# Attention scores in bursts of six PSUM banks instead of four, two bursts per head group

## The chip, the cores and the metric

One core of one Trainium2 chip. The metric is the device time of one execution in microseconds (us), the slowest (here the only) core, as the median of several runs.

## The reference

One transformer block, sequence 2048, width 1024, 32 heads of 32, a sliding window of 256 keys, bfloat16:

```python
q, k, v = split(layernorm(x) @ wqkv)                     # 32 heads of width 32
scores  = einsum("bhqd,bhkd->bhqk", q, k) * 32 ** -0.5
p       = softmax(where(0 <= q_idx - k_idx < 256, scores, -1e9))
h       = x + einsum("bhqk,bhkd->bhqd", p, v) @ wo
out     = h + silu(layernorm(h) @ w1) @ w2               # w1: 1024x3584, w2: 3584x1024
```

## The kernel before

The sequence is worked in four blocks of 512 queries. The attention of one block runs between the dense matmuls of the next one (its v, q and k projections; for the last block the output projection). Heads go in eight groups of four; the four heads of a group lie in the four 32-row tiles of the array (row tiles), which run at once: in the trace their four first score matmuls start within 0.01 us. A group needs 12 chunks of 128 keys by 128 queries per head, done in three bursts of four chunks:

```python
PIECES = {                                  # key tile, first query tile, how many, chunk
    "A": [(0, 0, 3, 0), (-2, 0, 1, 3)],
    "B": [(-1, 0, 2, 0), (2, 2, 2, 2)],
    "C": [(3, 3, 1, 0), (1, 1, 3, 1)],
}
def scores(b, g, kind):
    for kt, q0, nq, ch in PIECES[kind]:
        for hh in range(4):                 # four row tiles, each with a bank of its own
            r0 = hh * DH
            nc.tensor.matmul(sc[hh // 2][:, hh % 2, ch*P:(ch+nq)*P], lhsT=kT[...][r0:r0+DH, ...],
                             rhs=qT[b][r0:r0+DH, ...], start=True, stop=True, tile_position=(r0, 0))
    for pair in range(2):                   # one exponential per two heads: 1024 columns
        nc.scalar.activation(out=e, in_=sc[pair], func=ACT.Exp, scale=scale)
        ...                                 # masks on GpSimd
# ... per group g and kind:
    scores(b - 1, g, kind)
    dense[n]()                              # eight matmuls of 512 columns
    pending.pop(0)()                        # a third of the previous group's value matmuls
```

The kernel's PSUM tiles fill eight banks: four for scores, two accumulators, two for value outputs.

The softmax here doesn't subtract the row's maximum and nothing guards it: scores larger than these inputs give would overflow.

## Time and profile before

| what | measured |
|---|---|
| time, median of 3 | 696.83 us (696.65 to 697.57) |
| TensorE busy | 690.1 us, 99% of the span |
| one burst, first score to next dense matmul | 0.33 us |
| one head group (three dense groups, three bursts, 48 value matmuls), median | 7.68 us |
| bursts | 18 in the first attention block, 72 later |

In the profile's lines PE is TensorE's matmuls, PEld its weight loads, DVE VectorE, ACT ScalarE, POOL GpSimd. Read the timeline of TensorE by the starts: the end of a matmul is modelled, and one matmul lies over the next.

### The profile page before, as it was taken

How to read it: one execution, taken by the hardware profiler on the slowest of the kernel's cores; microseconds unless marked ns; L12 is line 12 of the kernel's file. 1: busy time of each engine (PE TensorE's matmuls, PEld its weight loads, DVE VectorE, ACT ScalarE, POOL GpSimd, SP SyncE). 2: the span in 40 equal slices, each digit the busy share in tenths (PEclk: the TensorE clock that was granted, in tenths of full speed). 3: DMA queues.
4: the chain of work that ended last, by engine and by line, in shares of the span. 5: the costliest groups of instructions: out<-in, count | busy, mean ns of one | idle time of the engine just before them, and what ended most of it. 6: DMA issues, size and time to landing. Idle time of an engine off the chain costs nothing.

```text
span 695.5 us, 12334 instructions
## 1 busy us (share of the span) xinstructions
PE 690.1 (99%) x5091; PEld 331.6 (48%) x5091; DVE 289.5 (42%) x616; ACT 257.9 (37%) x328; POOL 174.5 (25%) x391
## 2 busy tenths in 40 slices
PE   8999999999999999999999999999999999999998
PEld 3444444555555555544444444444444444444445
DVE  6267646644443448544316134433133251244111
ACT  4326657777777777621310023300033100233000
POOL 1007667777777777500000000000000000000000
PEclk9999999999999999999999999999999999999999
DMA  7732131026231778880123410024200023100110
GB/s 241 257 53 77 35 93 51 17 60 193 70 124 23 205 251 272 199 311 31 31 76 99 107 38 1 1 83 77 83 1 1 11 95 91 45 1 1 30 39 24
DMA packets 76457, 60.84 MB, mean 87 GB/s; under 512 B 50288, under 2 KB 60528, under 8 KB 76400
## 3 DMA queue, kind: packets, MB, share of 16 engines
q1 hardware_dynamic: 76256, 59.78, 29.9%
q8 instruction: 40, 0.66, 0.4%
q10 hardware_dynamic: 144, 0.26, 0.1%
q14 instruction: 17, 0.14, 0.1%
HBM read 39.85 MB, written 8.39 MB: 69 GB/s over the span
## 4 chain that ended last, share of the span: by engine, by line
PE 99%; DMA 1%; DVE 0%; issue 0%
PE hacc L563 19%; PE hacc L600 17%; PE acc L248 16%; PE acc L600 10%; PE acc L563 9%; PE acc L238 8%; PE acc L267 7%; PE o_ps L339 4%; PE sc L285 3%; PE hacc L267 1%; PE o_ps L354 1%; PE sc L313 1%; DMA r_o<-in_A_x_dram 1%; PE tp L216 0%; DVE ln_st L169 0%; DVE r_o L197 0%
## 5 line engine op out<-in xcount | busy, mean ns | idle before, releaser
L330 POOL TENSOR_SCALAR_AFFINE_SELECT r_e<-r_e 128x256 bf16<-128x256 bf16 (+1 forms) x384 | 171.6, 477 | 116.5 <-ACT r_e L322 65.1
L293 ACT ACTIVATE r_e<-sc 128x1024 bf16<-128x1024 f32 x144 | 139.5, 1021 | 45.1 <-PE sc L285 31.0
L600 PEld LDWEIGHTS <-r_a 128*128 128x128 bf16 x952 | 90.9, 98 | 103.0
L563 PEld LDWEIGHTS <-r_w 128*128 128x128 bf16 x896 | 87.4, 98 | 104.8
L600 PE MATMUL hacc<-r_a 128*128 128x512 bf16 (+2 forms) x616 | 122.5, 360 | 0.0
L563 PE MATMUL hacc<-r_e,r_w 128*128 128x512 bf16 x456 | 100.9, 379 | 0.0
L572 ACT ACTIVATE r_n<-hacc 128x512 f32<-128x512 f32 x30 | 17.9, 597 | 178.9 <-PE hacc L563 178.9
L600 PE MATMUL acc<-r_a 128*128 128x512 bf16 x336 | 74.0, 379 | 0.0
L248 PEld LDWEIGHTS <-r_w 128*128 128x128 bf16 x512 | 46.5, 97 | 57.1 <-issue 7.0
L250 DVE CAST r_a<-acc 128x512 bf16<-128x512 f32 x56 | 38.7, 691 | 72.9 <-PE acc L248 56.3
L248 PE MATMUL acc<-r_t,r_w 128*128 128x512 bf16 x256 | 60.0, 379 | 0.0
L248 PE MATMUL acc<-r_w 128*128 128x512 bf16 x256 | 58.2, 380 | 0.0
L267 PE MATMUL acc<-r_o,r_a 128*128 128x512 bf16 x208 | 49.4, 380 | 0.0
L563 PE MATMUL acc<-r_e,r_w 128*128 128x512 bf16 x216 | 49.1, 379 | 0.0
L339 PEld LDWEIGHTS <-r_e 128*128 128x128 bf16 x1152 | 39.5, 96 | 17.0
L322 ACT ACTIVATE r_e<-sc 128x1024 bf16<-128x1024 f32 x36 | 34.9, 1021 | 21.2 <-PE sc L313 20.1
L339 PE MATMUL o_ps<-r_a,r_e 128*128 128x33 bf16 x1152 | 40.2, 178 | 0.0
L615 DVE SCALAR_TENSOR_TENSOR r_t<-hacc,r_t 128x512 bf16<-128x512 f32 (+2 forms) x22 | 14.0, 635 | 56.7 <-PE hacc L600 56.7
L267 PEld LDWEIGHTS <-r_a 128*128 128x128 bf16 x256 | 23.1, 98 | 29.6 <-issue 5.1
L615 DVE SCALAR_TENSOR_TENSOR r_t<-acc,r_t 128x512 bf16<-128x512 f32 x12 | 8.3, 692 | 64.2 <-PE acc L600 64.2
L573 DVE SCALAR_TENSOR_TENSOR r_a<-r_n,hacc 128x512 bf16<-128x512 f32 x30 | 20.6, 688 | 33.0 <-ACT r_n L572 33.0
L563 PE MATMUL hacc<-r_a,r_w 128*128 128x512 bf16 x144 | 32.9, 379 | 0.0
(71 smaller groups left out, 476.5 us busy)
## 6 DMA issues: line engine op xcount, KB each, us to landing
r_w<-in_B_w_dram SPq DMA_DIRECT2D x8, 896.0 KB, 5.1
r_a<-in_B_w_dram SPq DMA_DIRECT2D x7, 1024.0 KB, 7.9
r_w<-in_A_wqkv_dram SPq DMA_DIRECT2D x6, 1024.0 KB, 8.7
h_dram<-r_t SPq DMA_DIRECT2D x16, 256.0 KB, 3.0
r_t<-h_dram SPq DMA_DIRECT2D x16, 256.0 KB, 2.8
out_dram<-r_t SPq DMA_DIRECT2D x31, 128.0 KB, 1.7
r_o<-in_A_x_dram SPq DMA_DIRECT2D x15, 256.0 KB, 4.0
r_e<-h_dram SPq DMA_DIRECT2D x3, 1024.0 KB, 5.7
```

What stands on the lines that cost most here:

```text
L238: nc.tensor.matmul(acc, lhsT=lnT_b[b % 2][:, kt, j * P:(j + 1) * P], rhs=wv[:, kt, c * 512:(c + 1) * 512], start=(kt == 0), stop=(kt == KT ...
L248: nc.tensor.matmul(acc, lhsT=wqk[:, kt, col0:col0 + P], rhs=lnT_b[b % 2][:, kt, :], start=(kt == 0), stop=(kt == KT - 1))
L250: copy(out=(qT, kT)[which][b][:, g, :], in_=acc)
L267: nc.tensor.matmul(acc, lhsT=qT[b][:, g, j * P:(j + 1) * P], rhs=wo[:, g, c * 512:(c + 1) * 512], start=(g == 0), stop=(g == G - 1))
L285: nc.tensor.matmul(sc[hh // 2][:, hh % 2, ch * P:(ch + nq) * P], lhsT=kT[t // 4][r0:r0 + DH, g, (t % 4) * P:(t % 4 + 1) * P], rhs=qT[b][r0 ...
L293: nc.scalar.activation(out=e, in_=sc[pair], func=ACT.Exp, scale=scale)
L322: nc.scalar.activation(out=e, in_=sc[pair], func=ACT.Exp, scale=scale)
L330: nc.gpsimd.affine_select(out=ap, in_=ap, pattern=[[0, 2], [0, n], [sgn, P]], compare_op=ALU.is_ge if upper else ALU.is_gt, fill=0.0, base ...
L339: nc.tensor.matmul(o_ps[pair][:, qt * 2 + hh, 0:VW], lhsT=e_of(i, kind, pair)[:, hh, ch * P:(ch + 1) * P], rhs=v[:, b * 4 + kt, g * 4 + pa ...
L563: nc.tensor.matmul(acc, lhsT=w1[:, kt, ft * P:(ft + 1) * P], rhs=ln2T[b][:, kt, :], start=(kt == 0), stop=(kt == KT - 1))
L600: nc.tensor.matmul(acc[:, 0:c1 - c0], lhsT=gT[:, ft, j * P:(j + 1) * P], rhs=w2[ft // 4][:, ft % 4, c0:c1], start=(ft == 0), stop=(ft == F ...
L615: nc.vector.scalar_tensor_tensor(out=t_out[j % 2][:, c0:c1], in0=acc[:, 0:c1 - c0], scalar=0.5, in1=t_in[j % 2][:, c0:c1], op0=ALU.mult, o ...
```

## The change

Its intent: every burst pays for switching the array into four row tiles and back, so fewer and longer bursts should cost less. A burst becomes six chunks per head (768 columns). The fifth and sixth go into half banks: heads 0 and 1 share the accumulator bank that is not in use, heads 2 and 3 one auxiliary bank taken from the value outputs. The design holds that two row tiles must not write one bank at once, so within a burst the odd heads write their halves first and the even heads last. What enforces it are two tiny "mark" matmuls: each takes a new tile of a pool with one buffer, so the second mark gets a semaphore wait (a semaphore is a counter that one instruction steps and another waits for) for the completion of the first.

```diff
+PIECES = [[(0,0,3,0), (-2,0,1,3), (-1,0,2,4)], [(3,3,1,0), (1,1,3,1), (2,2,2,4)]]
-    if not bursts or len(bursts[-1]) == 4:
+    if not bursts or len(bursts[-1]) == 6:
+    half = [acc[:, 0:256], acc[:, 256:512], flat[:, 0:256], flat[:, 256:512]]
+    for hh in range(4):
+        at = 0
+        for p in (aux + own[::-1] if hh % 2 else own):      # odd heads: auxiliary first
+            todo.append((at, 1 - hh % 2, hh, p)); at += p[4]
+    todo.sort(key=lambda t: t[:3])
+    def mark(hh):
+        nc.tensor.matmul(o_tile()[:, 0, 0:4], lhsT=ident[r0:r0+DH, :], rhs=ident[r0:r0+DH, 0:4],
+                         start=True, stop=True, tile_position=(r0, 0))
+    for _, _, hh, p in todo:
+        if hh == 1 and p[5] < 4 and not marked:
+            mark(1); marked = True
+        score(hh, p)
+    mark(0)
+    for p in aux:
+        for hh in (0, 2):                                   # even heads: auxiliary last
+            score(hh, p)
+    exp(ea[:, 0:2, :], acc); exp(em[:, 0, :], sc[0][:]); exp(em[:, 2, :], sc[2][:])
+    exp(ea[:, 2:4, :], flat); exp(em[:, 1, :], sc[1][:]); exp(em[:, 3, :], sc[3][:])
 ... (cut: masks on four heads at once, one value output bank in place of two, value matmuls
 ...  in two pieces per group, bursts after the 7th and 4th matmul of a dense group,
 ...  layernorm statistics in half steps)
```

## The prediction

> **What bounds the kernel now.** I read the engine totals first, then the chain of waits that ended last, then the timeline inside one attention stage. The totals and the chain by line:
>
> ```profile
> PE 690.1 (99%) x5091; PEld 331.6 (48%) x5091; DVE 289.5 (42%) x616; ACT 257.9 (37%) x328; POOL 174.5 (25%) x391
> ...
> PE 99%; DMA 1%; DVE 0%; issue 0%
> ```
>
> TensorE (PE) is never without a matmul in flight and the chain is PE from end to end. So only PE's own stream counts, plus any new wait put into it. But "busy" also covers the drain of the array between kinds of matmul, so the timeline must tell what is stream and what is drain. One iteration of the output-projection stage, with ScalarE beside it:
>
> ```profile
> 242.06 0.40 PE L285 MATMUL sc<-r_a 32*128 32x128 bf16 x8
> ...
> 242.39 1.90 PE L267 MATMUL acc<-r_o,r_a 128*128 128x512 bf16 x8
> ...
> 242.58 1.94 ACT L293 ACTIVATE r_e<-sc 128x1024 bf16<-128x1024 f32 x2 [0.67 <-PE sc L285]
> ...
> 244.13 0.54 PE L339 MATMUL o_ps<-r_a,r_e 128*128 128x33 bf16 x15
> ...
> 244.60 0.40 PE L285 MATMUL sc<-r_a 32*128 32x384 bf16 x8
> ```
>
> Columns: start and duration in us, engine, line, operation, how many. Read starts, not durations: the ends are modelled. Scores to dense group: 0.33 us. Eight dense matmuls to the value matmuls: 1.74 us, so 0.216 each. Fifteen value matmuls to the next scores: 0.47 us. The piece after 290.16 (value matmuls, then dense at 290.54) has the same fifteen in 0.38 us, so one value matmul costs 0.025 us and the way from full-array work into the scores costs about 0.09 us. The scores stream 512 columns on each of four row tiles at once; at the dense rate that is 0.213 us, so the way out of the scores costs 0.33 - 0.213 = 0.12 us. The first attention block, where scores interrupt a dense stream, agrees:
>
> ```profile
> 59.83 2.53 PE L238 MATMUL acc<-r_w,r_t 128*128 128x512 bf16 x11
> ...
> 62.29 0.40 PE L313 MATMUL sc<-r_a 32*128 32x128 bf16 x12
> ...
> 62.63 0.62 PE L354 MATMUL o_ps<-r_a,r_e 128*128 128x33 bf16 x18
> ...
> 63.09 2.53 PE L238 MATMUL acc<-r_w,r_t 128*128 128x512 bf16 x11
> ```
>
> Eleven dense matmuls are 2.37 us, and 62.29 - 59.83 = 2.46: again 0.09 into the scores. From 62.63 to 63.09 is 0.46 us for eighteen: going from value to dense work costs 0.01. So **each burst of scores pays 0.21 us of switching whatever its length.** A head group of three iterations should then take 24 x 0.2157 + 48 x 0.025 + 3 x (0.213 + 0.21) = 5.18 + 1.20 + 1.27 = 7.65 us; the three later stages (106.9 to 290.6 us, 24 groups) measure 7.65. No stall is hidden in them. The MLP part (about 405 us) is dense matmuls at full rate, which the change leaves alone.
>
> **What the Trainium skill says.** TensorEngine Tiling (Array Packing), section Key Properties: changing the tiling mode drains the array. The trace agrees, with 0.09 us in and 0.12 us out. The same page, Gotcha 1: different row tiles cannot access one PSUM bank at the same time, and software has to keep them apart. No run yet shows it, but it is what the marks are for: heads 0 and 1 now share an accumulator bank, 2 and 3 the auxiliary bank. TensorE: Matmul & The Clock Gate, section Back-to-back issue gap: N/2.4 + 2.5 ns, with a floor near 25 ns. The trace has 0.216 us for N = 512 and 0.025 us for 33 columns. ScalarE: Activation LUTs, section What ACT_TABLE_LOAD costs: 186 ns plus 0.833 ns an element, about 93 ns of it overlapped back to back. The trace has 597 ns at 512 elements, 1021 at 1024, and 1.94 us for a pair, so an overlap of 0.10.
>
> **The change, part by part.**
>
> (a) Removed: one burst of three per head group (24 groups in the later blocks), and 6 of 18 in the first block. The columns stay the same (3 x 512 = 2 x 768). Gain: 24 x 0.21 + 6 x 0.21 = 6.3 us. All of it lies on PE's path.
>
> (b) Added: order within a burst. Odd heads write their auxiliary half (256 columns) first, even heads last. Matmuls issue in order. Row tile 1: auxiliary 0 to 0.107 us, mark (0.025), 128 columns, then 384 columns from 0.185. Tile 0: 384 columns to 0.168, its last 128 queued behind tile 1's and thus 0.19 to 0.24; then the mark of tile 0, and its auxiliary half to about 0.375. A full overlap would end at 0.32. So 0.055 us a burst is lost even if nothing waits: 60 bursts x 0.055 = 3.3 us.
>
> (c) Added: the mark of tile 0 reuses the one output tile and so should wait until the mark of tile 1 has completed, a wait of PE upon itself. A value matmul shows about 0.18 us from start to modelled end, and the first weight load behind a VectorE result starts some 0.06 us after that result. Tile 1's mark starts at 0.107, so the wait opens at about 0.107 + 0.17 + 0.06 = 0.34 us; if completions are in order (the 384-column matmuls ahead of it show 0.326 us) at about 0.40. Without it the mark would go at 0.24. So the wait costs 0.10 to 0.16 us a burst: 60 x 0.10 to 0.16 = 6 to 9.6 us.
>
> (d) ScalarE: six exponentials of 512 per burst in place of two of 1024. By 0.597 and the 0.10 overlap, six in a row take 3.08 us, and two bursts 6.2 us of a group's 7.5; before, 3 x 1.94 = 5.8. The tight place is from the second burst of a group to the first of the next: 4 dense + 24 value + 7 dense matmuls are 0.86 + 0.61 + 1.51 us, with switching 3.2 us. The last bank is free about 0.30 + 3.08 + 0.05 = 3.43 us after the burst's stream ends (0.30: from the end of the score stream, 242.06 + 0.21, to the activation at 242.58), and is wanted 0.13 us into the next burst, at 3.33. A stall of up to 0.1 us per group, 24 x 0.1 = 2.4 us, or none.
>
> (e) Single output bank: the normalisation (0.2 + 0.42 us on VectorE, behind a 0.69 us cast) must end before the next mark. It ends about 0.95 us after the value matmuls, the mark comes 1.6 us after: hidden. Splitting the statistics into halves of about 0.65 us keeps VectorE from delaying those casts. GpSimd masks: per group 4 of 256 and 6 of 512 elements a partition by the new lists, counting the two auxiliary ones:
>
> ```profile
> L330 POOL TENSOR_SCALAR_AFFINE_SELECT r_e<-r_e 128x256 bf16<-128x256 bf16 x288 | 116.8, 423 | 95.1 <-ACT r_e L322 65.1 <-ACT r_e L293 26.7
> L330 POOL TENSOR_SCALAR_AFFINE_SELECT r_e<-r_e 128x512 bf16<-128x512 bf16 x96 | 61.2, 637 | 21.4 <-ACT r_e L293 21.4
> ```
>
> 423 and 637 ns each (mean in the column after busy time), so 5.5 us, under the group's 7.5, and hidden unless the last mask of a burst is late.
>
> (f) Moved: value matmuls in two pieces of 24 rather than three of 15 to 18: 0.01 us each, nothing. The second layernorm's steps move from whole tiles to halves, on engines with idle time: nothing.
>
> **Sum.** Without a PE self-wait: -6.3 + 3.3 = -3.0 us, 694. With it: -6.3 + 3.3 + 6 to 9.6 = +3 to +6.6 us, and up to +2.4 for ScalarE: 700 to 706.
>
> **Rivals.**
> 1. *The wait is cheap or not there.* Then about 694. For it: the order of heads plainly places the first mark early and the second late, and the whole kernel has been fitted round it (bursts after seven and after four dense matmuls), which suggests that it pays. Against: PE's long pipe, 0.17 us even for a tiny matmul.
> 2. *The self-wait eats the saving.* About 700 to 703. For it: the arithmetic of (c). Against: (c) takes a modelled matmul end for the real one.
> 3. *ScalarE becomes the bound in the attention stages.* If its six exponentials did not overlap, they would need 3.6 us per burst plus the turn-round of about 0.7: 8.6 us a group, 24 x 0.95 = 23 us more, 720. Against: pairs overlap now, although each has its own semaphores.
>
> **Range and chances.** I give rival 1 a little over half, since the saving of (a) is measured and the size of (c) is not, rival 2 some 40%, rival 3 about 4%. The point is 696 us, between the first two; the range that holds it 8 times in 10 is 691 to 704. Faster by over 2% would need 683 us, and the most that the burst count can give is 6.3 us: 0.02. Slower by over 2% needs 711, so rival 3: 0.04. Within 2%: 0.94.
>
> **What would show it right or wrong.** In the timeline of the changed kernel: first score to next dense matmul 0.44 us when perfect, 0.50 without the wait, 0.60 or more with it; and a late start of the auxiliary matmuls of heads 0 and 2 in that burst. The group's length over a stage: 7.5 us (rival 1) or 7.75 (rival 2). ScalarE's runs of six at about 3.1 us, and whether PE's score group follows directly upon their end (step d). The prediction is wrong if the switching cost depends on burst length, if accumulator or output banks make dense matmuls wait, or if masks arrive late for the value matmuls: each would show as a gap of PE starts outside the score bursts.

## The result, and the profile after

705.86 us (705.26 to 706.02, 4 runs) against 696.74 us for the kernel before in the same rounds (4 runs): 9.1 us slower. The ratio is 1.0127, 95% interval 1.0109 to 1.0144. Ratios here are the mean time of one kernel's fast runs over that of the other's fast runs of the same rounds, so not quite the ratio of the medians. The result is within 2%, as forecast, but outside the range of 691 to 704.

The engine totals and the chain of the changed kernel:

```profile
PE 692.6 (98%) x5119; PEld 335.4 (48%) x5219; DVE 295.0 (42%) x616; ACT 266.1 (38%) x508; POOL 165.5 (24%) x331
...
PE 96%; DVE 1%; issue 1%; DMA 1%; ACT 0%; POOL 0%; ACTq 0%; POOLq 0%
```

TensorE is still the bound. The totals do not tell where 9 us went. The busy time seems to grow by 2.5 us only, but 100 matmul records are missing from this trace (5119 matmuls beside 5219 weight loads; before, 5091 of each): some 95 gaps of 0.05 us, 5 us in all, come of that, and experiment 5, where no record is missing, has none of them. And a wait that is shorter than the modelled tail of the matmul before it does not show as idle time. The timeline of TensorE alone through one burst does (start us, length us, engine, line, operation, count):

```profile
180.77 0.38 PE L249 MATMUL acc<-r_w,r_t 128*128 128x512 bf16 x1
181.08 0.28 PE L311 MATMUL acc<-r_a 32*128 32x256 bf16 x1
181.09 0.28 PE L311 MATMUL o_aux<-r_a 32*128 32x256 bf16 x1
181.09 0.33 PE L311 MATMUL sc<-r_a 32*128 32x384 bf16 x2
181.20 0.16 PE L321 MATMUL o_ps<-ident 32*128 32x4 bf16 x1
181.23 0.38 PE L311 MATMUL sc<-r_a 32*128 32x128 bf16 x6
181.52 0.16 PE L321 MATMUL o_ps<-ident 32*128 32x4 bf16 x1
181.53 0.28 PE L311 MATMUL o_aux<-r_a 32*128 32x256 bf16 x1
181.54 0.27 PE L311 MATMUL acc<-r_a 32*128 32x256 bf16 x1
181.74 0.39 PE L249 MATMUL acc<-r_w,r_t 128*128 128x512 bf16 x1
```

The two marks are the rows of L321. The first starts 0.12 us into the burst, the second at 0.44. Tile 0's own 512 columns are 0.21 us of stream at the dense rate. Only after the second mark do the even heads' auxiliary columns start, and the next dense matmul comes 0.66 us after the first score. A burst before took 0.33. Two of 0.66 are 1.32 us where three of 0.33 were 0.99; one way into the scores is saved (0.09 in the prediction), which leaves 0.24 us a group.

By the traces: the median head group went from 7.68 to 7.92 us, so 24 groups give 6.0 us. One burst of the last stage also waits 0.5 us for VectorE to read an accumulator. The first attention block gives about 1.8 us. The part after the last burst gives about 0.7 us, of which 0.40 is a value piece that starts before its mask is there (experiment 8). The spans of the two profiles differ by 8.9 us, so this is all of it within the rounding.

### The profile page after: what moved, and what is told of

Same layout as the page of the kernel before. It is cut to its first block, busy times and chain, and to the rows that moved or that the text cites. A ratio compares the mean times of both kernels' runs of the same rounds, so it can differ in the third digit from the quotient of the medians.

```text
span 704.4 us, 12771 instructions
## 1 busy us (share of the span) xinstructions
PE 692.6 (98%) x5119; PEld 335.4 (48%) x5219; DVE 295.0 (42%) x616; ACT 266.1 (38%) x508; POOL 165.5 (24%) x331
## 4 chain that ended last, share of the span: by engine, by line
PE 96%; DVE 1%; issue 1%; DMA 1%; ACT 0%; POOL 0%; ACTq 0%; POOLq 0%
PE sc L594 18%; PE sc L631 17%; PE acc L259 15%; PE acc L631 10%; PE acc L594 9%; PE acc L249 8%; PE acc L280 6%; PE o_ps L387 5%; PE sc L311 2%; PE acc L311 2%; PE sc L280 1%; PE o_aux L311 1%; PE o_aux L176 1%; DMA r_t<-r_o 1%; PE o_ps L321 1%
## 5 line engine op out<-in xcount | busy, mean ns | idle before, releaser
L355 POOL TENSOR_SCALAR_AFFINE_SELECT r_e<-r_e 128x512 bf16<-128x512 bf16 (+1 forms) x324 | 162.6, 537 | 136.2 <-ACT r_e L337 136.2
L337 ACT ACTIVATE r_e<-sc 128x512 bf16<-128x512 f32 x240 | 132.2, 619 | 0.0
L631 PE MATMUL sc<-r_a 128*128 128x512 bf16 (+2 forms) x604 | 121.8, 359 | 0.6
L594 PE MATMUL sc<-r_e,r_w 128*128 128x512 bf16 x441 | 100.1, 379 | 0.8
L603 ACT ACTIVATE r_n<-sc 128x512 f32<-128x512 f32 x30 | 17.9, 597 | 178.9 <-PE sc L594 128.3
L337 ACT ACTIVATE r_e<-acc 128x512 bf16<-128x512 f32 x60 | 35.8, 597 | 68.4 <-PE acc L311 46.4
L387 PE MATMUL o_ps<-r_a,r_e 128*128 128x33 bf16 x1440 | 46.6, 178 | 0.1
L311 PEld LDWEIGHTS <-r_a 32*128 32x128 bf16 x752 | 20.9, 91 | 35.7 <-issue 34.7
L646 DVE SCALAR_TENSOR_TENSOR r_t<-sc,r_t 128x512 bf16<-128x512 f32 (+2 forms) x22 | 14.0, 635 | 55.6 <-PE sc L631 55.6
L337 ACT ACTIVATE r_e<-o_aux 128x512 bf16<-128x512 f32 x60 | 37.1, 618 | 0.0
```

The source lines that it names most:

```text
L311: return nc.tensor.matmul(dst, lhsT=kT[t // 4][r0:r0 + DH, g, (t % 4) * P:(t % 4 + 1) * P], rhs=qT[b][r0:r0 + DH, g, q0 * P:q0 * P + cols] ...
L337: return nc.scalar.activation(out=out, in_=in_, func=ACT.Exp, scale=scale)
L355: nc.gpsimd.affine_select(out=ap, in_=ap, pattern=[[0, e.shape[1]], [0, n], [sgn, P]], compare_op=ALU.is_ge if upper else ALU.is_gt, fill= ...
L387: nc.tensor.matmul(o[:, qt * 2 + hh % 2, 0:VW], lhsT=e, rhs=v[:, b * 4 + kt, g * 4 + hh, :], start=(kt == parts[0][0]), stop=(kt == qt),)
L594: nc.tensor.matmul(acc, lhsT=w1[:, kt, ft * P:(ft + 1) * P], rhs=ln2T[b][:, kt, :], start=(kt == 0), stop=(kt == KT - 1))
L603: nc.scalar.activation(out=th, in_=acc, func=ACT.Tanh, scale=0.5)
```

## The experiments

Theory A: the wait of the second mark for the first costs the time. Rivals: B, the longer bursts overload ScalarE, GpSimd or the shared accumulator; C, the tiny matmuls themselves; and the order of heads, which the prediction charged with 0.055 us a burst. Experiments 1 to 4 ran on one chip beside the kernel before (696.31 us, 696.26 to 696.73), 5 and 6 beside 696.67, 7 and 8 beside 696.75 (one run of the kernel before there, of 793.11 us, was slow and is left out). Each has four timed runs, and each edit is against the changed kernel.

**1. No shared bank, no marks, plain order** (wrong output).

```diff
-  dst = ... half[hh][:, ...]                                   # for chunks 4 and 5
+  dst = ... (half[hh] if hh % 2 else sc[hh])[:, ...]           # even heads: over their own bank
-  (ordered loop with marks)
+  for p in own + aux:
+      for hh in range(4):
+          score(hh, p)
```

> Wrong output on purpose: heads 0 and 2 write their auxiliary columns over their own score bank, so no two row tiles share a bank; no marks, no turn, plain order over the four heads. Everything else as in the changed kernel. Theory A (the turn, order plus self-wait, costs the time): a burst takes 0.44 us from the first score to the next dense matmul where the changed kernel took 0.66, 60 bursts x 0.22 = 13 us less: about 692 us, faster than the kernel before (696.8). Rival B (the longer bursts overload ScalarE, GpSimd or the shared accumulator bank): 703 us or more, with gaps outside the bursts.

697.13 us, ratio to before 1.0009 (0.9994 to 1.0024). Neither: 8.7 us faster than the changed kernel, but 5 slower than A expected. The trace says where they are. The burst ahead of the value matmuls, TensorE's rows:

```profile
175.75 0.53 PE L311 MATMUL sc<-r_a 32*128 32x384 bf16 x8
176.02 0.27 PE L311 MATMUL acc<-r_a 32*128 32x256 bf16 x1
176.02 0.29 PE L311 MATMUL sc<-r_a 32*128 32x256 bf16 x2
176.16 0.27 PE L311 MATMUL o_aux<-r_a 32*128 32x256 bf16 x1
176.36 0.39 PE L249 MATMUL acc<-r_w,r_t 128*128 128x512 bf16 x1
```

and what ScalarE did just before:

```profile
174.77 1.12 ACT L331 ACTIVATE r_e<-sc 128x512 bf16<-128x512 f32 x2
```

ScalarE's last two exponentials end at 175.89. Single records show three of the first four matmuls starting within 0.02 us of 175.75 and the fourth, which needs the bank that the last exponential frees, at 175.94. The first burst of a group takes 0.61 us (median), the second 0.44. This is the wait of step d of the prediction, with the bank wanted at the burst's start instead of 0.13 us into it.

**2. The order of the changed kernel, no marks** (wrong output; even heads over their own bank as in 1).

```diff
   for _, _, hh, p in todo:
-      if hh == 1 and p[5] < 4 and not marked: mark(1); marked = True
       score(hh, p)
-  mark(0)
```

> Wrong output on purpose, as the first of this set, but in the order of the changed kernel (odd heads' auxiliary columns first, even heads' last), without marks. A, step b of the prediction: 0.055 us a burst for the order alone, so 3.3 us above the first of this set, about 695. Rival: the order alone costs most of the 13 us (703 or more).

692.30 us (692.03 to 692.54), ratio 0.9941 (0.9925 to 0.9958): faster than the kernel before.

```profile
176.83 0.28 PE L311 MATMUL acc<-r_a 32*128 32x256 bf16 x1
176.83 0.28 PE L311 MATMUL o_aux<-r_a 32*128 32x256 bf16 x1
176.84 0.50 PE L311 MATMUL sc<-r_a 32*128 32x384 bf16 x10
177.27 0.39 PE L249 MATMUL acc<-r_w,r_t 128*128 128x512 bf16 x1
```

From first score to dense matmul 0.44 us, in both bursts of the group: 768 columns in full overlap (0.32) plus 0.12 out. The order costs nothing, and ScalarE's wait is gone. The reason is an earlier start of the exponentials: with the odd heads' auxiliary columns first, and the even heads' kept out of that bank, the first exponential starts 0.37 us into a burst (median) where experiment 1 has 0.63. So the last one ends 0.11 us before the next group's first burst, where in experiment 1 it ends 0.15 us after that burst's start:

```profile
172.12 0.64 ACT L333 ACTIVATE r_e<-sc 128x512 bf16<-128x512 f32 x1
172.87 0.28 PE L311 MATMUL acc<-r_a 32*128 32x256 bf16 x1
```

It is the reverse of what was expected: below experiment 1, not above it. A median group takes 7.48 us against 7.68. So the saving of the intent is real, though here with exponentials that start earlier than in the changed kernel (0.81 us into the burst).

**3. Marks that do not wait** (wrong output).

```diff
   (as 2, with both marks in place)
-  nc.tensor.matmul(o_tile()[:, 0, 0:4], lhsT=ident[...], ...)
+  nc.tensor.matmul(sc[hh][:, 0:4], lhsT=ident[...], ...)
```

> Wrong output on purpose, as the second of this set, with both mark matmuls in their places, but each written to its own head's score bank, so that neither waits for the other. A: the mark matmuls cost at most 0.03 us a burst, so 695 to 697, and the remaining 9 to 11 us up to the changed kernel (705.9) are the wait of the second mark for the first. Rival C (the small extra matmuls with new weights are what costs): 703 or more.

693.19 us (692.78 to 693.83), ratio 0.9954. The mark matmuls cost 0.9 us in all; C falls.

```profile
178.28 0.28 PE L311 MATMUL acc<-r_a 32*128 32x256 bf16 x1
...
178.40 0.16 PE L321 MATMUL sc<-ident 32*128 32x4 bf16 x1
...
178.51 0.16 PE L321 MATMUL sc<-ident 32*128 32x4 bf16 x1
...
178.74 1.04 PE L249 MATMUL acc<-r_w,r_t 128*128 128x512 bf16 x4
```

The second mark starts 0.23 us into the burst instead of 0.44, and the burst takes 0.46 instead of 0.66. This kernel and the changed one differ in whether the second mark waits, and in the bank that the even heads' columns go to. The bank costs nothing: from the second mark to the next dense matmul is 0.22 us in both. 705.86 - 693.19 = 12.7 us over 60 bursts is 0.21 us a burst; in the trace the second mark and the end of the burst move by 0.20. (The two kernels were timed in different sets, in which the kernel before differs by 0.4 us.)

**4. One more wait.**

```diff
   mark(0)
+  mark(2)
   for p in aux: ...
```

> Right output. The changed kernel with one more mark in the turn, from row tile 2 and in the same output tile, between the mark of tile 0 and the auxiliary columns: one more wait of TensorE upon itself per burst. A: the wait runs its full length here, 0.17 for the tiny matmul's pipe plus about 0.08 for the semaphore, 60 x 0.25 = 15 us more, about 721 us. B or C: a few us more, under 709.

Correct, 718.22 us (717.82 to 718.53): 12.4 us above the changed kernel, 0.21 us a burst for one further wait, where 0.25 was expected.

```profile
175.38 0.28 PE L311 MATMUL acc<-r_a 32*128 32x256 bf16 x1
...
175.50 0.16 PE L321 MATMUL o_ps<-ident 32*128 32x4 bf16 x1
...
175.81 0.37 PE L321 MATMUL o_ps<-ident 32*128 32x4 bf16 x2
176.03 0.28 PE L311 MATMUL acc<-r_a 32*128 32x256 bf16 x1
...
176.25 1.04 PE L259 MATMUL acc<-r_w 128*128 128x512 bf16 x4
```

The row with x2 holds the second and third mark; the auxiliary matmul behind them starts at 0.65 us instead of 0.45. So the wait of TensorE on itself, doubled, doubles its cost: A stands. B falls as the cause of the 9 us, since experiments 2 and 3 keep the longer bursts and are faster than the kernel before.

**5 and 6. Can the signal come earlier?** From mark to waiting mark is 0.32 us in the changed kernel, 0.21 in experiment 4, where no long matmul stands just before the first of the two. 5 issues the first mark before the even heads' 384 columns. 6 does so as well, and puts it on row tile 2, which is idle then.

```diff
+  for p in aux:
+      for hh in (1, 3): score(hh, p)
+  mark(1)                       # 5;   mark(2) in 6
   for _, _, hh, p in todo:
-      if hh == 1 and p[5] < 4 and not marked: ...
+      if p[5] < 4:
           score(hh, p)
   mark(0)
```

> Right output. The changed kernel with the mark of tile 1 issued directly after the odd heads' auxiliary matmuls and ahead of the even heads' 384 columns. In the changed kernel the second mark starts 0.32 us after the first; in the third-mark run, where no long matmul stands before the mark, 0.21. Theory D (completions come in order, so the first mark's signal waits for the 384-column matmuls issued just before it): the second mark starts 0.09 to 0.11 us earlier, bursts of about 0.57 instead of 0.66 us, 60 x 0.09 = 5 us less: 700 to 702 us. Rival E (the wait has a fixed length, whatever stands before): even heads start later, nothing gained: 705 to 709.

> Right output. As the early mark, but the first mark runs on row tile 2, which is idle, so it need not wait for tile 1's 256 columns to pass. D: its completion still comes after that of the auxiliary matmuls before it (0.28 us after the burst's start by the modelled end), so the second mark starts at about 0.33, bursts of 0.58 us, 60 x 0.08 = 5 us less than the changed kernel: 700 to 702. Rival F (a mark signals as soon as it is itself through): second mark at 0.23, no wait, bursts of 0.46 us: about 693, which would beat the kernel before.

Both correct: 703.55 us (703.43 to 703.62) and 703.46 (703.26 to 703.53), ratio 1.0091 both. A gain of 2.3 to 2.4 us instead of 5, and the same for both; rival E, no gain, falls. Experiment 6:

```profile
175.75 0.28 PE L311 MATMUL acc<-r_a 32*128 32x256 bf16 x1
...
175.76 0.17 PE L321 MATMUL o_ps<-ident 32*128 32x4 bf16 x1
175.76 0.49 PE L311 MATMUL sc<-r_a 32*128 32x384 bf16 x8
176.15 0.16 PE L321 MATMUL o_ps<-ident 32*128 32x4 bf16 x1
```

Its first mark starts 0.01 us into the burst, ends (modelled) at 0.18, and still the second mark goes only at 0.40. F falls. The trace also holds the steps of TensorE's own semaphore, and they tell why. In the changed kernel it stepped at 0.361 and 0.395 us, and the second mark started at 0.439; the two 384-column matmuls issued ahead of the first mark end, by the model, at 0.340 and 0.343. In 5 it stepped at 0.295, 0.329 and 0.363, and the second mark started at 0.405; the auxiliary matmuls ahead of the mark end at 0.280 and 0.284. So signals come in program order, here 0.034 us apart, and the waiting matmul starts 0.04 us after the one it needs. In 6 a 384-column matmul issued behind the mark ends by the model at 0.366, after the mark's signal at 0.363, so the mark does not wait for what comes behind it. Moving the mark took the 384-column matmuls from its front (theory D), but the compiled program of 5 and 6 lets each auxiliary matmul signal too, and two signals at 0.034 us gave most of the gain back.

Can such a turn pay at all? A group of two bursts takes 7.48 us with bursts of 0.44 and must stay under 7.68, so a burst may take 0.44 + 0.10 = 0.54 us; 6 has 0.62. An estimate: if only the mark signalled, the second mark would go 2 x 0.034 earlier and the burst would take 0.56. That still loses, so it was not built. No correct version here beats the kernel before. Leaving the wait out with the shared banks in place was not tried: nothing would order the two row tiles on one bank.

**7. Was it ScalarE in experiment 1?** (Wrong output.)

```diff
   (as 1)
-  exp(ea[:, 2:4, :], flat)
+  exp(ea[:, 2:3, 0:64], flat[:, 0:64])
+  nc.gpsimd.memset(r_e[:, 2048:12288], 1.0)     # once, at the start; and masks fill with 1
```

> Wrong output on purpose. The own-bank run (697.1 us beside 692.3 for the odd-first order, both without a turn) with one of the six exponentials cut from 512 to 64 columns; the buffers start at 1 and masks fill with 1 so that no sum is zero. Theory G (in the own-bank run the fourth head's first matmul waits in each group for ScalarE's six exponentials: it starts 0.19 us after the other three): the exponentials are 0.37 us shorter, the wait goes, 24 x 0.17 = 4 us less, about 693 us. Rival H (four row tiles starting together on six banks cost time by themselves): stays at 697.

700.77 us in all, 3.6 above experiment 1, so the total misses. But the added memset runs in the first stage (8.94 us on GpSimd), four normalisations on VectorE beside it stretch from 1.12 to 7.06 us, and TensorE waits for them: the first dense matmul of the second block starts at 57.37 us instead of 50.33, 7.0 us later. The stages of interest behave as G said. The burst that took 0.61 us is 0.44:

```profile
181.36 0.50 PE L312 MATMUL sc<-r_a 32*128 32x384 bf16 x9
181.59 0.27 PE L312 MATMUL acc<-r_a 32*128 32x256 bf16 x1
...
181.80 0.39 PE L250 MATMUL acc<-r_w,r_t 128*128 128x512 bf16 x1
```

and the median group went from 7.66 to 7.49 us. 700.8 - 7.0 = 693.7, near the 693 expected; H falls. So the chain of six exponentials is what held experiment 1 up.

**8. The value pieces left for the MLP part, one matmul group later.**

```diff
-  if extra:
+  if extra and ft >= 1:
       extra.pop(0)[0]()
```

> Right output. The changed kernel with the two value pieces left over for the MLP part issued one group of matmuls later. In the changed kernel the first of them waits 0.56 us there for a mask (its 24 matmuls took 1.17 us to the modelled end instead of 0.61). Theory: that wait goes, 0.5 us less, 705.3 us. Rival: the wait is hidden or moves, no difference.

Correct, 704.83 us (704.75 to 705.46), ratio to before 1.0116 (1.0098 to 1.0134). That is 1.0 us below the changed kernel's median of another set of rounds, but the intervals of the two ratios overlap, so by the times alone it is unclear. The trace is clear: the piece of 24 value matmuls that stretched over 1.17 us now takes 0.76, and the part after the last burst takes 406.5 us instead of 406.9. By starts the wait was 0.40 us (1.01 us to the next dense matmul instead of 0.61), not the 0.56 of the expectation, which set a modelled end against a time between starts. First the changed kernel, then this one:

```profile
300.69 1.17 PE L387 MATMUL o_ps<-r_a,r_e 128*128 128x33 bf16 x24
```

```profile
302.26 0.76 PE L387 MATMUL o_ps<-r_a,r_e 128*128 128x33 bf16 x24
```

## Why the prediction was wrong

- **(a), fewer switches: right in kind, a little large.** It said 6.3 us. Experiment 2, which has the longer bursts without the turn, gains 4.0 us of it; its median group gains 0.19 us where 0.21 was expected. Two waits for VectorE before bursts of its last stage (1.7 us in its trace) and the stretched value piece are among what is missing. The 7.65 us that the prediction measured for a group leaves out the first burst; from burst to burst it is 7.67, 0.02 above its sum.
- **(b), the order of heads: wrong.** It said matmuls issue in order, so the even heads' last 128 columns would queue behind the odd heads' and cost, with the mark behind them, 0.055 us a burst. Measured: 0.44 us a burst without the marks, as short as the plain order of experiment 1, and 0.46 with them. Row tiles did not wait for one another's turn in program order: in experiment 5 the two 384-column matmuls, issued after the first mark, start at 0.01 us, the mark at 0.12.
- **(c), the self-wait: the mechanism right, the size short, and then left out of the point. This is the step that failed.** It said 0.10 to 0.16 us a burst, 6 to 9.6 us in all, and the point of 696 took it as more likely that the wait is cheap or hidden (rival 1). Measured: 0.21 us a burst and 12.7 us (from experiment 3 to the changed kernel). For completions in order the text put the start of the second mark at 0.40, and it was 0.44. Its 0.06 us from a modelled end to the start that waits for it holds (0.018 to the signal, 0.044 from there to the start). What it lacked is the signal ahead of the mark's own, 0.034 us; the rest is that the 384-column matmul ahead ends at 0.34 us, not 0.326.
- **(d), ScalarE: sound.** It said up to 0.1 us a group, or none. In the changed kernel it is none: the last exponential ends 0.12 us into the burst (median), and the second mark is waited for until 0.44 anyway. Experiments 1 and 7 show the wait where the bank is wanted at the burst's start: 0.17 us a group.
- **(e) and (f):** VectorE, GpSimd masks and the single output bank cost nothing visible inside the groups of the first two of the later stages: the group of experiment 2 is as short as its matmuls. Not foreseen: the wait of 0.5 us for VectorE in the last stage, and that of the first value piece in the MLP part for its mask, 0.40 us.
- **The sum and the choice.** The measured terms are -4.0 (longer bursts), +0.9 (marks) and +12.7 us (wait), together +9.6. They are differences of successive runs and so must add up; against the kernel before of the result's own rounds it is 9.1. The prediction had worked out 700 to 706 for rival 2, and 705.86 lies in it, but by luck: its 3.3 us for (b) and 2.4 for (d), mostly not paid, make up for what (c) lacked. It then set its point at 696 because the kernel "plainly" arranges the marks to hide the wait. That was an argument from intent against a number read from the trace, and it cost the range.

## What to carry to other kernels

A wait of TensorE on its own earlier matmul is not free ordering: it costs the whole pipe and the signal, here 0.21 us each time, and what is issued behind it waits too, on the other row tiles as well: head 2's auxiliary columns start up to 0.03 us after tile 0's mark, never before it. Before adding one, compare it with what it buys: here 0.10 us per burst. And when a blind estimate has a number for a new wait, a design that looks as if it hides the wait is no reason to halve it.

## What the Trainium skill lacked or had wrong

- TensorE: Matmul & The Clock Gate, section The mechanism, says that matmuls are strictly first in, first out in start and in end. Across row tiles the starts were not: in experiment 5 two matmuls start at 0.013 and 0.016 us, a matmul ahead of them in the kernel's order at 0.122; in the changed kernel the even heads' last 128 columns start at 0.18 us, an odd head's 384 columns, ahead of them, at 0.20. The signals do keep program order: in the changed kernel a 128-column matmul that ends by the model at 0.398 us signals at 0.563, after a 384-column one of 0.531.
- The same page, section The cost: per-tile semaphore tail, gives 26.3 ns for each increment and 4.7 ns for each tile. The serial steps measured here are 34 ns apart (0.295, 0.329, 0.363 us).
- No page has the cost of a TensorE wait on its own completion: 0.21 us from a tiny matmul to the next that waits for it, plus what longer matmuls stand before it (0.32 us in the changed kernel).
- TensorEngine Tiling (Array Packing), section Key Properties, has the drain on a change of mode but no size: here 0.10 us into four row tiles from dense work (0.31 from last dense matmul to first score, less 0.216) and 0.12 us out.
